# Routing of an attention-then-experts kernel: two-operand work moved from VectorE to GpSimd or PSUM, and a new order of the last head pair

## The chip, the cores and the metric

The kernel runs on one core of a Trainium2 chip. The core has a matrix engine (TensorE, PE), a vector engine (VectorE, DVE), an activation engine (ScalarE, ACT), GpSimd (POOL) and a DMA queue that SyncE issues (SP). All run their own instruction queue in order and wait for each other by semaphores. The metric is device time of one execution in microseconds.

## The reference, cut to what matters

```python
# attention: 4 batches, 8 heads, 768 tokens, 64 dims; a query sees only keys with the same 6-bit hash
mask = q_bucket[:, :, :, None] == k_bucket[:, :, None, :]
scores = where(mask, scale * q @ k.T, -1e9)
attn_out = softmax(scores) @ v                      # -> x of 3072 tokens x 512
# mixture of experts: 8 experts, the best one of each token
logits = x @ w_gate
expert_idx = argmax(logits, axis=1)
gate_w = softmax(logits)[arange(N), expert_idx]
# for each expert e: y[its tokens] = relu(x[its tokens] @ w1[e]) @ w2[e]
return gate_w[:, None] * y
```

The argmax takes the first of equal logits, and the weight of the chosen expert is 1 over the sum of exp(logit - maximum).

## The kernel before, in words

**Stages.** Attention runs over 16 pairs of heads (4 batches of 4 pairs), then the experts run as dense matrix products over rows that were sorted by expert in DRAM. A pair's work is cut into named steps, and a table of tokens sets their order: `HEAD` for the first pair, `PLAN` for each of the next 14, `LAST` for the sixteenth. All engines get their instructions in the order of the tokens, so a token that waits on an engine holds all later tokens of that engine.

**Tokens.** A token's digits name a unit; each trailing `-` means the pair before. `S` scores (PE, into a PSUM bank named `s`, 3 banks), `R` minimum and copy of the scores (DVE, L307), `X` exponential (ACT, L313), `T` four transposes on PE (L327) into a bank named `t` (2 banks, shared by `T`, `V`, `K`, `G` and routing), `E` their eviction (`a` on ACT, `v` on DVE), `V` product with the values (PE, L389, 24 instructions), `O` its eviction (ACT, L395), `M` the reciprocal sums (DVE), `K` tokens and logits (PE, L409), `L` their scaling into the row buffer `xr` (DVE, L419), `D` half the transposes of the weights on DVE (L349), `G` the hash products of the next pair (PE, L254), `H` their signs (ACT), `N` the load of the hash masks (two DMAs issued by POOL, L270), `P0` to `P7` the split of the next pair's queries and keys into a high and a low part (POOL, L190 to L200). The scores of a pair need the masks and the split parts that the pair before it made.

**Routing.** A batch's four pairs give the logits (summed over pairs in L441). `route` then finds the maximum, the first index that has it, a one-hot row `oh`, and on PE (L460 to L463) running counts that give each token its slot in the sorted rows. Batches 0 to 2 route all six token tiles in one generator, a step at a time: `route_step` runs steps 1 to 6 behind the `R` tokens of the second pair of the next batch (from `L0--` on: `R0 R3 R11 R10 R5 R4`), steps 7 and 8 at `G` of its third pair, two more behind the first `R`s there. The last batch runs in two halves of three tiles inside `LAST`, by tokens `r0` and `r1`; its result decides the order of experts.

**The end of attention.** In `LAST` POOL (and a little ACT) also splits the first expert's weights, 16 parts of a cast (`n`) and a subtraction (`t`), some by tokens and some behind `R` tokens; two raw buffers are loaded by SP after each second subtraction. `x0` and `x2` transpose 256 early rows of the first expert, `g` and `h` evict them to a high (ACT) and a low part (DVE, L755), `m0` to `m7` are the first product with those rows (PE, L772, 12 matmuls each), `u` and `d` its ReLU and low part, `c0` and `c1` the scatter of the last batch's rows (POOL). Each `m` reads the quarters of `x0` first and those of `x2` from its seventh matmul on.

Of the kernel before, what the change touches and what calls it, by code (L numbers as in the profile page):

```python
# [7 lines left out]
F32 = mybir.dt.float32  # L8
# [23 lines left out]
M0 = float(2 ** 34)  # L32
# [22 lines left out]
def lsh_attention_moe(ctx, tc, qk, qk2, v, proj, wg, w1, w1p, w2, out):  # L55
    nc = tc.nc
    const = ctx.enter_context(tc.tile_pool(name="const", bufs=1))
    moe = ctx.enter_context(tc.tile_pool(name="moe", bufs=1))
    ps = ctx.enter_context(tc.tile_pool(name="ps", bufs=1, space=bass.MemoryType.PSUM))
    ctx.enter_context(tc.manual_schedule())  # L60
    attn = ExitStack()
    wk = attn.enter_context(tc.tile_pool(name="wk", bufs=2))
# [73 lines left out]
    C = {}  # L136
# [244 lines left out]
    PV, RC, OT, LT, XR = {}, {}, {}, {}, {}  # L381
# [47 lines left out]
    def route(b, hfs):

        nt = 3 * len(hfs)
        l = wk.tile([128, 2, 2 * 3, E], F32, name="rl")
        lg, eq = l[:, 0, :nt], l[:, 1, :nt]
        f = wk.tile([128, 3, 2 * 3], F32, name="rf")
        mx, fi, sm = f[:, 0, :nt], f[:, 1, :nt], f[:, 2, :nt]
        oh = C["oh"] if nt > 3 else C["ohs"][:, hfs[0]]
        ex = C["ex"][:, 3 * hfs[0]:3 * hfs[0] + nt]
# [21 lines left out]
        p = ps.tile([128, 512], F32, name="t", bufs=2)  # L459
# [5 lines left out]
        yield  # L465
        pb = wk.tile([128, 2 * 3 + 1, E], F32, name="pb")
        nc.vector.tensor_tensor(pb[:, :nt + 1], p[:, :(nt + 1) * E].rearrange("p (t e) -> p t e", e=E),
                                C["base"][:, None, :].to_broadcast([128, nt + 1, E]), op=OP.add)
        C["base"] = pb[:, nt]
        pb = pb[:, :nt]  # L470
        yield
        nc.vector.tensor_tensor(pb, pb, oh[:, :nt], op=OP.mult)
        slot = wk.tile([128, 2 * 3], I32, name="slot")
        with nc.allow_low_precision("whole numbers below 2**24"):
            nc.vector.tensor_reduce(slot[:, :nt], pb, axis=AX.X, op=OP.add)
        yield
        nc.vector.tensor_reduce(sm, ex, axis=AX.X, op=OP.add)
        for i, hf in enumerate(hfs):
            nc.vector.reciprocal(XR[b, hf][:, :, GC], sm[:, 3 * i:3 * i + 3])
            SL[b, hf] = slot[:, 3 * i:3 * i + 3]  # L480
        yield

    def scatter(b, hf):
# [297 lines left out]
    M1 = {}  # L781
# [104 lines left out]
    routes, parts, pick = {}, list(range(16)), pick_first()  # L886
# [10 lines left out]
    def weight_half(op, x):  # L897
# [48 lines left out]
    steps = dict.fromkeys(range(B - 1), 0)  # L946

    def on(b, n):
        for _ in range(n):
            next(routes[b], None)  # L950
            steps[b] += 1

    def route_step(g, w, k):

        b, q = divmod(g - NP, NP)
        if 0 <= b < B - 1 and w[0] == "R" and q == 1 and {(g - 2, "L0"), (g - 2, "L1")} <= DONE and steps[b] < 6:
            if b not in routes:
                routes[b] = route(b, (0, 1))
# [44 lines left out]
    def step(g, w):  # L1003
# [173 lines left out]
    with tc.If(C["n"] > 0):  # L1177
        with tc.For_i(0, C["n"], 1) as i:
# [16 lines left out]
            p = ps.tile([128, 512], F32, name="t", bufs=2)  # L1195
# [5 lines left out]
            for f in range(8):  # L1201
                p = ps.tile([128, 512], F32, name="t", bufs=2)
# [3 lines left out]
            p = ps.tile([128, 512], F32, name="s", bufs=3)  # L1206
# [34 lines left out]
```

## Time and profile before

| | us |
|---|---|
| median of 3 timed runs | 717.16 (716.2 to 717.37) |
| profiled execution, its own time | 715.56 |
| its span, first to last instruction | 713.7 |
| PE busy in the span | 695.7 |
| DVE, ACT, POOL busy | 454.3, 434.9, 469.0 |
| mean granted TensorE clock | 0.993 |

The profile is of one execution. "Busy" of PE means that an instruction was in flight, so a PE that runs at half clock is busy too. The span stands 1.9 us under that execution's own time, and its own time 1.6 us under the median of the timed runs.

### The profile page before, as it was taken

Reading aid. Unit: us, or ns where it says so; the run is one execution under the profiler, and the core shown is the slowest. Engines: PE = TensorE matmul, PEld = TensorE weight load, DVE = VectorE, ACT = ScalarE, POOL = GpSimd, SP = SyncE. Lnnn points to the kernel's source line nnn. Section 1 sums busy time; section 2 is a strip of 40 time slices with the busy share of each in tenths; the row PEclk is TensorE's granted clock in tenths of the full one; section 3 lists DMA queues with packets and bytes.
Section 4 is the critical chain, followed back from the end, with each engine's and each line's share of the span. In section 5 each row is a group of like instructions: output and inputs, shape, how many; then the busy total and the mean of one; then the engine's idle time right before and its main releaser. Section 6 shows DMA issues by size and latency. Waiting matters only on the chain.

```text
span 713.7 us, 12263 instructions
## 1 busy us (share of the span) xinstructions
PE 695.7 (97%) x4219; PEld 568.3 (80%) x4219; DVE 454.3 (64%) x924; ACT 434.9 (61%) x864; POOL 469.0 (66%) x507
## 2 busy tenths in 40 slices
PE   9999999899999999998999799999999999999997
PEld 5777768667686668676876599899999999989896
DVE  8878777977788878788864632641848534262521
ACT  7988788668888788887866214543444444444320
POOL 7966855565796658874967704766656667768432
PEclk9999999899999999999999999999999999999999
DMA  8519867866888448865875218584537495637201
GB/s 306 130 53 247 223 208 215 219 160 213 258 234 225 130 135 227 220 201 117 241 236 186 100 65 227 174 229 128 162 113 186 137 114 214 192 133 215 75 11 40
DMA packets 64528, 123.09 MB, mean 172 GB/s; under 512 B 15331, under 2 KB 29027, under 8 KB 64400
## 3 DMA queue, kind: packets, MB, share of 16 engines
q1 hardware_dynamic: 56736, 103.17, 52.1%
q0 software_dynamic: 7584, 19.10, 8.5%
q8 instruction: 34, 0.56, 0.3%
q14 instruction: 30, 0.25, 0.1%
q10 hardware_dynamic: 144, 0.02, 0.0%
HBM read 65.75 MB, written 26.33 MB: 129 GB/s over the span
## 4 chain that ended last, share of the span: by engine, by line
PE 89%; issue 4%; DVE 3%; ACT 1%; POOL 1%; DMA 0%; POOLq 0%; ACTq 0%; DVEq 0%
PE s L772 18%; PE t L389 18%; PE s L809 10%; PE s L297 10%; PE t L327 10%; PE s L299 9%; PE s L829 8%; PE t L409 3%; PE t L254 2%; PE s L838 1%; DVE e L307 1%; POOL w L668 1%; DVE rl L448 1%; PE t L103 1%; ACT e L313 0%
## 5 line engine op out<-in xcount | busy, mean ns | idle before, releaser
L307 DVE TENSOR_SCALAR_CACHE_REDUCE e<-s 128x768 f32<-128x768 f32 x192 | 178.7, 954 | 62.0 <-PE s L299 54.5
L313 ACT ACTIVATE e<-e,m 128x768 f32<-128x768 f32 x192 | 177.9, 930 | 17.4 <-DVE e L307 14.8
L668 POOL TENSOR_TENSOR w<-raw,w 128x512 fp32r<-128x512 f32 x112 | 144.7, 1319 | 38.7 <-ACT w L667 38.2
L389 PE MATMUL t<-pt,vt 128*64 128x384 f32 x768 | 131.3, 491 | 0.0
L772 PE MATMUL s<-xh,w 128*128 128x456 f32 (+6 forms) x672 | 126.8, 346 | 0.0
L772 PEld LDWEIGHTS s<-xh,w 128*128 128x128 f32 x672 | 119.2, 188 | 3.1
L788 DVE SCALAR_TENSOR_TENSOR hh<-s,hh 128x256 fp32r<-128x256 f32 (+7 forms) x64 | 35.5, 555 | 110.7 <-ACT hh L786 103.8
L389 PEld LDWEIGHTS t<-pt,vt 128*64 128x64 f32 x768 | 52.4, 137 | 64.3 <-issue 63.2
L327 PE MATMUL t<-ident,e 128*128 128x128 f32 x648 | 93.5, 276 | 3.9 <-DVE xr L419 2.7
L379 ACT ACTIVATE pt<-t 128x512 f32<-128x512 f32 (+1 forms) x149 | 83.3, 582 | 19.4 <-PE t L327 18.2
L327 PEld LDWEIGHTS t<-ident,e 128*128 128x128 f32 x648 | 77.6, 142 | 11.7 <-issue 4.4
L786 ACT ACTIVATE hh<-s 128x256 fp32r<-128x256 f32 (+7 forms) x64 | 31.4, 490 | 88.5 <-PE s L772 83.5
L349 DVE STREAM_TRANSPOSE w<-e 128x768 f32<-128x768 f32 x84 | 79.2, 965 | 0.2 <-ACT e L313 0.2
L809 PE MATMUL s<-hh,w 128*128 128x456 f32 (+3 forms) x384 | 74.9, 355 | 0.0
L809 PEld LDWEIGHTS s<-hh,w 128*128 128x128 f32 x384 | 71.1, 188 | 2.6
L667 ACT ACTIVATE w<-raw 128x512 fp32r<-128x512 f32 x112 | 66.3, 622 | 6.5 <-DMA raw<-in_w1p_dram 6.5
L845 POOL DMA_INDIRECT out_dram<-y,ix x26 | 25.9, 997 | 61.7 <-DVE y L843 30.9
L297 PE MATMUL s<-w 80*128 80x384 f32 x192 | 56.2, 374 | 2.9 <-DVE e L307 2.9
L829 PE MATMUL s<-w,hh 128*128 128x512 f32 (+1 forms) x240 | 56.4, 394 | 0.0
L297 PE MATMUL s<-qk 80*128 80x384 f32 x192 | 54.8, 367 | 0.0
L829 PEld LDWEIGHTS s<-w,hh 128*128 128x128 f32 (+1 forms) x240 | 44.6, 187 | 10.5
L299 PE MATMUL s<-w 128*128 128x384 f32 x192 | 50.1, 342 | 0.0
(206 smaller groups left out, 995.0 us busy)
## 6 DMA issues: line engine op xcount, KB each, us to landing
pt<-w SPq DMA_DIRECT2D x224, 144.0 KB
raw<-in_w_dram SPq DMA_DIRECT2D x36, 512.0 KB
raw<-in_w1p_dram SPq DMA_DIRECT2D x28, 512.0 KB
xd<-in_qk_dram SPq DMA_DIRECT2D x14, 768.0 KB
sorted_rows<-xr SPq DMA_DIRECT2D x6, 1156.0 KB
vt<-in_v_dram SPq DMA_DIRECT2D x16, 384.0 KB
masks<-bits POOLq DMA_DIRECT2D x14, 192.0 KB, 3.9
sorted_rows<-sorted_rows SPq DMA_DIRECT2D x2, 1156.0 KB
```

The source lines that it names most:

```text
L297: nc.tensor.matmul(p[:, a, :HALF], k[0:80, 2, c], k[0:80, 3, n], start=i >= 4, stop=i < 4)
L299: nc.tensor.matmul(p[:, a, :HALF], k[:, 0, c], k[:, 1, n], start=i < 4, stop=i >= 4)
L307: nc.vector.tensor_scalar(e, SC.pop(i)[:, :, :HALF], CEIL, None, op0=OP.min, op1=OP.min, accum_out=m)
L313: nc.scalar.activation(e, e, AF.Exp, bias=m, scale=-1.0, accum_out=SM[g, hf][:, t, s:s + 1])
L327: nc.tensor.transpose(o[:, j, w], e[w][:, kt // 3, (kt % 3) * 128:(kt % 3) * 128 + 128], ident)
L349: nc.vector.transpose(z[:, :, c, w].rearrange("p g (k i) -> p g k i", i=32), e)
L379: nc.scalar.activation(o, x, AF.Copy)
L389: nc.tensor.matmul(p[s * 64:(s + 1) * 64, :HALF], VT[g][:, kt, s, :], PT[u][:, :, :, s, kt].rearrange("p a t i -> p t a i"), start=(kt == ...
L668: nc.gpsimd.tensor_tensor(w[:, 1, a], r, w[:, 0, a], op=OP.subtract)
L772: nc.tensor.matmul(p[:, :c], w[:, a, d, fs], x[:, b, d, :c], start=(k == 0), stop=(k == 11))
L809: nc.tensor.matmul(p[:, :c], w[:, a, f % 4, ms], h[b][:, f, :c], start=(k == 0), stop=(k == 23))
L829: nc.tensor.matmul(p[:pw], HH[n][b][:, f, i:i + pw], w[:, a, f % 4], start=(k == 0), stop=(k == 23))
```

## The change

Batches 0 to 2: `route` gives to POOL every step that combines two SBUF operands. The one-hot row comes from a subtraction and a comparison with zero (`zero`) in place of a comparison of two tensors. Five small instructions go to POOL behind the maximum and behind `fi`, and one (`pb` times `oh`) behind the counts; DVE keeps the reductions and the addition that reads PSUM. The exponential and the counts stand at `G`, and the steps are one more.

The last batch: `route_last` keeps all on DVE and puts the logits, `eq` and `fi` in the unused part of the counts' PSUM bank, so that each two-operand instruction has one operand in PSUM.

`LAST` is a new table of the same work: `x2 g2 h2 m6 m1` move ahead of `L1` and `r1`, the half that pair 15 finishes first is `K0 L0`, `K1` stands right behind `V1`, two subtractions of the weights move from POOL to DVE (`tV`), and one part of the weights to the end.

```diff
+        def zero(o, x):
+            G.tensor_scalar(o, x, 0.0, 1.0, op0=OP.is_equal, op1=OP.mult)
+        logits(b, 0, lg[:, 0:3])
+        yield
+        logits(b, 1, lg[:, 3:6])
         nc.vector.tensor_reduce(mx, lg, axis=AX.X, op=OP.max)
-        nc.vector.tensor_tensor(eq, lg, bc(mx), op=OP.is_equal)
-        nc.vector.tensor_tensor(eq, eq, dsc, op=OP.mult)
+        yield
+        G.tensor_tensor(lg, lg, bc(mx), op=OP.subtract)
+        zero(eq, lg)
+        G.tensor_tensor(eq, eq, dsc, op=OP.mult)
+        yield
+        yield
+        yield
         nc.vector.tensor_reduce(fi, eq, axis=AX.X, op=OP.max)
-        nc.vector.tensor_tensor(oh[:, :nt], dsc, bc(fi), op=OP.is_equal)
-        (nc.gpsimd if many else nc.vector).tensor_tensor(lg, lg, bc(mx), op=OP.subtract)
+        G.tensor_tensor(eq, dsc, bc(fi), op=OP.subtract)
+        zero(oh[:, :nt], eq)
         yield
         nc.scalar.activation(ex[:, :, 0:E], lg, AF.Exp)
-        yield
         p = ps.tile([128, 512], F32, name="t", bufs=2)
+        counts(p, oh, nt)
+        yield
...
+        C["base"] = pb[:, nt]
+        G.tensor_tensor(pb[:, :nt], pb[:, :nt], oh[:, :nt], op=OP.mult)
...
+    def route_last(b, hf):
+        nt = 3
+        p = ps.tile([128, 512], F32, name="t", bufs=2)
+        part = [p[:, (nt + 1 + i) * E * nt:(nt + 2 + i) * E * nt].rearrange("p (t e) -> p t e", e=E) for i in range(3)]
+        lg, eq = part[:2]
+        fi = part[2][:, :, 0]
...
+        logits(b, hf, lg)
+        V.tensor_reduce(mx, lg, axis=AX.X, op=OP.max)
+        yield
+        V.tensor_tensor(eq, lg, bc(mx), op=OP.is_equal)
+        V.tensor_tensor(eq, eq, dsc, op=OP.mult)
+        V.tensor_reduce(fi, eq, axis=AX.X, op=OP.max)
+        V.tensor_tensor(oh[:, :nt], dsc, bc(fi), op=OP.is_equal)
+        yield
+        V.tensor_tensor(l, lg, bc(mx), op=OP.subtract)
+        nc.scalar.activation(ex[:, :, 0:E], l, AF.Exp)
+        yield
+        counts(p, oh, nt)
...
+        V.tensor_tensor(q[:, :nt], q[:, :nt], C["base"][:, None, :].to_broadcast([128, nt, E]), op=OP.add)
+        V.tensor_tensor(q[:, :nt], q[:, :nt], oh[:, :nt], op=OP.mult)
+        slots(b, (hf,), q[:, :nt])
...
     LAST = """
-        r0 r0 r0 r0 r0 r0 c0 x2 O1 K1 L1 r1 r1 r1 r1 r1 r1 r1 c1 g2 h2 m6 m3 u3 d3 m2 u2 d2 m7 u6 d6 u7 d7 m1 u1 d1 m4
+        R7 E42a T50 E50a T52 E52v K0 L0 nP tV x0 X7 T31 E31a T30 T32 E30a M1 E32v K0- g0 h0 V1 O1 K1 nP tP nA tP L0-
+        r0 r0 r0 r0 r0 r0 c0 x2 g2 h2 m6 u6 m1 u1 L1 r1 r1 r1 r1 r1 d6 r1 c1 d1 m7 u7 d7 m3 u3 d3 m4 u4 d4 m2 u2 d2 m0
...
-            elif w[0] == "R" and 8 <= steps[b] < 10:
+            elif w[0] == "R" and 8 <= steps[b] < 11:
                 on(b, 1)
```

DVE in the second pair of the second batch, between the logits and the eviction that follows; L307 is an `R`, L349 a `D`, L419 an `L`. Before:

```order
L441 TENSOR_REDUCE rl<-xr 128x24
L349 STREAM_TRANSPOSE w_1587<-e 128x4x192 x3
L307 TENSOR_SCALAR e,m<-s 128x768
L444 TENSOR_REDUCE rf<-rl 128x6
L445 TENSOR_TENSOR rl<-rl,rf 128x48
L307 TENSOR_SCALAR e,m<-s 128x768
L448 TENSOR_TENSOR rl<-rl,desc 128x48
L451 TENSOR_REDUCE rf<-rl 128x6
L419 TENSOR_TENSOR xr<-t,r 128x3x144
L307 TENSOR_SCALAR e,m<-s 128x768
L454 TENSOR_TENSOR oh<-desc,rf 128x48
```

And after the change, in the same place:

```order
L477 TENSOR_REDUCE rl<-xr 128x24
L446 TENSOR_REDUCE rf<-rl 128x6
L349 STREAM_TRANSPOSE w_1588<-e 128x4x192 x3
L307 TENSOR_SCALAR e,m<-s 128x768 x2
L419 TENSOR_TENSOR xr<-t,r 128x3x144
L307 TENSOR_SCALAR e,m<-s 128x768 x2
L454 TENSOR_REDUCE rf<-rl 128x6
```

L445, L448 and L454 left DVE; of the rows that remain only L419 has two operands, and one of them (`t`) is in PSUM. The maximum comes earlier, and the reduction to `fi` stands two `R`s later.

POOL in the same pair, from the last cast before the masks to the pair's end: before (the first three rows of the split, then the routing's one subtraction, the masks and the low parts `P3 P2 P7`):

```order
L198 TENSOR_TENSOR qk<-xd,qk 64x768
L194 CAST qk<-xd 64x768
L196 COPY qk<-qk 64x768
L455 TENSOR_TENSOR rl<-rl,rf 128x48
L270 DMA qk<-masks 16x4x384 x2
L200 TENSOR_TENSOR qk<-xd,qk 64x768
L198 TENSOR_TENSOR qk<-xd,qk 64x768
L200 TENSOR_TENSOR qk<-xd,qk 64x768
L194 CAST w_1790<-xd 64x768
```

After:

```order
L198 TENSOR_TENSOR qk<-xd,qk 64x768
L448 TENSOR_TENSOR rl<-rl,rf 128x48
L441 TENSOR_SCALAR rl<-rl 128x48
L450 TENSOR_TENSOR rl<-rl,desc 128x48
L194 CAST qk<-xd 64x768
L196 COPY qk<-qk 64x768
L455 TENSOR_TENSOR rl<-desc,rf 128x48
L441 TENSOR_SCALAR oh<-rl 128x48
L270 DMA qk<-masks 16x4x384 x2
L200 TENSOR_TENSOR qk<-xd,qk 64x768
L198 TENSOR_TENSOR qk<-xd,qk 64x768
L200 TENSOR_TENSOR qk<-xd,qk 64x768
```

Three small instructions stand behind the maximum, and two behind `fi`; the masks and the three low parts stand behind those two. Behind the last L200 follows the product of `pb` and `oh`, ahead of the next pair's first cast.

PE at the end of attention, from the last `V` on (L389 is `V1`, L409 a `K`, L460 and L463 the counts, L751 is `x2`, L772 an `m`); before:

```order
L327 MATMUL t<-ident,e 128x4x32 x12
L409 MATMUL t<-wgt,ot 128x144 x3
L389 MATMUL t<-pt,vt 64x384 x12
...
L463 MATMUL t<-ohs,ones 128x8
L751 MATMUL s<-ident,xd 128x128 x4
L409 MATMUL t<-wgt,ot 128x144 x3
...
L463 MATMUL t<-ohs,ones 128x8
L772 MATMUL s<-xhe,w_4428 128x256 x12
```

After (the counts are L480 and L482, `x2` is L801, an `m` L822):

```order
L327 MATMUL t<-ident,e 128x4x32 x12
L409 MATMUL t<-wgt,ot 128x144 x3
L389 MATMUL t<-pt,vt 64x384 x12
L409 MATMUL t<-wgt,ot 128x144 x3
...
L482 MATMUL t<-ohs,ones 128x8
L801 MATMUL s<-ident,xd 128x128 x4
L822 MATMUL s<-xhe,w_4401 128x256 x12
L822 MATMUL s<-xhe,w_4308 128x256 x12
...
L482 MATMUL t<-ohs,ones 128x8
L822 MATMUL s<-xhe,w_4401 128x256 x12
```

`K1` moved ahead of the first half's counts, and two `m`s (24 matmuls) stand between the two counts where `K1` alone stood.

## Rows read from the trace of the kernel before

**Rows 1.** Waits of PE: waited for, us in total, times, longest us.

```profile
PE s L297 <- DVE e L307: 2.9, 2, 1.6
PE t L460 <- DVE ohs L454: 2.8, 2, 2.4
PE t L327 <- DVE xr L419: 2.7, 1, 2.7
PE s L772 <- DVE xhe L755: 1.1, 1, 1.1
```

**Rows 2.** The chain in order of time: start us, us, what (`V1`, `G`, `V0`).

```profile
102.39 4.02 PE t L389 x24
118.91 0.78 PE t L254 x8
125.47 4.02 PE t L389 x24
154.85 4.02 PE t L389 x24
238.16 4.02 PE t L389 x24
242.75 0.85 PE t L254 x8
318.60 4.02 PE t L389 x24
344.20 4.02 PE t L389 x24
```

**Rows 3.** Windows: us, PE, PEld, DVE, ACT, POOL busy, PE clock, DMA, GB/s.

```profile
137.00:144.00 7.00, 6.04 (x24) 5.24 (x26) 6.04 (x14) 4.47 (x10) 2.62 (x2) 0.51 0.36 79
407.00:410.00 3.00, 2.60 (x12) 2.60 (x13) 0.35 (x1) 0.00 (x0) 2.18 (x5) 0.50 0.52 190
```

**Rows 4.** Tile rl: DVE's product, duration ns min/median/max, first and last start.

```profile
L448 DVE TENSOR_TENSOR rl<-rl,desc x5: 182/205/4169, 132.9 to 404.3; 128x48 f32<-128x48 f32 x3, 128x24 f32<-128x24 f32 x2
L455 POOL TENSOR_TENSOR rl<-rl,rf x3: 268/268/270, 131.9 to 325.0; 128x48 f32<-128x48 f32 x3
```

**Rows 5.** Timeline of DVE and POOL in batch 2's routing: start us, us.

```profile
328.03 2.60 DVE L454 TENSOR_TENSOR oh<-desc,rf 128x48 bf16<-128x48 f32 x1
...
326.90 1.86 POOL L200 TENSOR_TENSOR qk<-xd,qk 64x768 fp32r<-64x768 f32 x1
328.71 1.83 POOL L198 TENSOR_TENSOR qk<-xd,qk 64x768 fp32r<-64x768 f32 x1
```

**Rows 6.** Timeline of a pair without routing: DVE's `R4`, POOL's `N`.

```profile
111.77 0.95 DVE L307 TENSOR_SCALAR_CACHE_REDUCE e<-s 128x768 f32<-128x768 f32 x1
...
105.30 1.02 POOL L270 DMA_DIRECT2D w<-masks  x2
```

**Rows 7.** The masks' load, line 270: us from issue to landing.

```profile
DMA to landing us min/median/max: 3.2/4.1/4.6
```

**Rows 8.** Timeline of the last pair's end, each engine: start us, us.

```profile
389.18 4.00 PE L327 MATMUL t<-ident,e 128*128 128x128 f32 x24
407.40 12.18 PE L772 MATMUL s<-xhe,w 128*128 128x256 f32 x89 [1.14 <-DVE xhe L755]
...
389.29 0.49 ACT L395 ACTIVATE ot<-t 128x384 f32<-128x384 f32 x1 [1.13 <-PE t L389]
405.19 0.58 ACT L753 ACTIVATE xhe<-s 128x512 fp32r<-128x512 f32 x1
...
406.67 0.68 DVE L755 TENSOR_TENSOR xhe<-s,xhe 128x512 fp32r<-128x512 f32 x1
...
377.65 0.61 POOL L908 CAST w<-raw 128x512 fp32r<-128x512 f32 x1 [4.72 <-DMA raw<-in_w_dram]
399.48 1.27 POOL L665 TENSOR_TENSOR w<-raw,w 128x512 fp32r<-128x512 f32 x1
...
374.87 0.89 SPq L694 DMA_DIRECT2D xd<-sorted_rows  x2
```

More of the change, by code (lines that the diff above doesn't have):

```diff
@@ L427, in bc, with route @@
         return ap[:, :, None].to_broadcast([128, ap.shape[1], E])
[L429 to L431 removed]
+    def route(b):
+        nt = 6
         l = wk.tile([128, 2, 2 * 3, E], F32, name="rl")
[L433 removed]
+        lg, eq = l[:, 0], l[:, 1]
         f = wk.tile([128, 3, 2 * 3], F32, name="rf")
[L435 to L437 removed]
+        mx, fi, sm = f[:, 0], f[:, 1], f[:, 2]
+        oh, ex = C["oh"], C["ex"]
@@ L458, in route @@
+        counts(p, oh, nt)
         yield
-        p = ps.tile([128, 512], F32, name="t", bufs=2)
+        pb = wk.tile([128, 2 * 3 + 1, E], F32, name="pb")
+        nc.vector.tensor_tensor(pb, p[:, :(nt + 1) * E].rearrange("p (t e) -> p t e", e=E),
+                                C["base"][:, None, :].to_broadcast([128, nt + 1, E]), op=OP.add)
+        C["base"] = pb[:, nt]
+        G.tensor_tensor(pb[:, :nt], pb[:, :nt], oh[:, :nt], op=OP.mult)
+        yield
+        nc.vector.tensor_reduce(sm, ex, axis=AX.X, op=OP.add)
@@ L460, in route, with logits, counts @@
+        for i in range(2):
+            nc.vector.reciprocal(XR[b, i][:, :, GC], sm[:, 3 * i:3 * i + 3])
+        yield
+        yield
+        slots(b, (0, 1), pb[:, :nt])
+        yield
+    def logits(b, hf, o):
+        nc.vector.tensor_reduce(o, XR[b, hf][:, :, :GC].rearrange("p t (a x e) -> p t e a x", a=NP, e=E)[:, :, :, :, 0:PW // E:PW // E - 1], axis=AX.XY, op=OP.add)
+    def counts(p, oh, nt):
         nc.tensor.matmul(p[:, :(nt + 1) * E], C["tri"], oh, start=True, stop=False)
@@ L464, in route, with slots @@
                              start=False, stop=(t == nt - 1))
[L465 to L472, printed above, removed]
+    def slots(b, hfs, pb):
@@ new lines, in slots @@
+        for i, hf in enumerate(hfs):
+            SL[b, hf] = slot[:, 3 * i:3 * i + 3]
+    def route_last(b, hf):
+        nt = 3
+        p = ps.tile([128, 512], F32, name="t", bufs=2)
+        part = [p[:, (nt + 1 + i) * E * nt:(nt + 2 + i) * E * nt].rearrange("p (t e) -> p t e", e=E) for i in range(3)]
+        lg, eq = part[:2]
+        f = wk.tile([128, 3, 2 * 3], F32, name="rf")
+        mx, sm = f[:, 0, :nt], f[:, 2, :nt]
+        fi = part[2][:, :, 0]
+        l = wk.tile([128, 2, 2 * 3, E], F32, name="rl")[:, 0, :nt]
+        oh = C["ohs"][:, hf]
+        ex = C["ex"][:, 3 * hf:3 * hf + nt]
+        dsc = C["desc"][:, None, :].to_broadcast([128, nt, E])
+        V = nc.vector
+        logits(b, hf, lg)
+        V.tensor_reduce(mx, lg, axis=AX.X, op=OP.max)
+        yield
+        V.tensor_tensor(eq, lg, bc(mx), op=OP.is_equal)
+        V.tensor_tensor(eq, eq, dsc, op=OP.mult)
+        V.tensor_reduce(fi, eq, axis=AX.X, op=OP.max)
+        V.tensor_tensor(oh[:, :nt], dsc, bc(fi), op=OP.is_equal)
+        yield
+        V.tensor_tensor(l, lg, bc(mx), op=OP.subtract)
+        nc.scalar.activation(ex[:, :, 0:E], l, AF.Exp)
+        yield
+        counts(p, oh, nt)
+        yield
+        q = p[:, :(nt + 1) * E].rearrange("p (t e) -> p t e", e=E)
+        if hf == 0:
+            pb = wk.tile([128, 2 * 3 + 1, E], F32, name="pb")
+            V.tensor_tensor(pb[:, nt], q[:, nt], C["base"], op=OP.add)
+        V.tensor_tensor(q[:, :nt], q[:, :nt], C["base"][:, None, :].to_broadcast([128, nt, E]), op=OP.add)
+        if hf == 0:
+            C["base"] = pb[:, nt]
+        V.tensor_tensor(q[:, :nt], q[:, :nt], oh[:, :nt], op=OP.mult)
+        slots(b, (hf,), q[:, :nt])
+        yield
+        V.tensor_reduce(sm, ex, axis=AX.X, op=OP.add)
+        V.reciprocal(XR[b, hf][:, :, GC], sm)
@@ L957, in route_step @@
             if b not in routes:
[L958 removed]
+                routes[b] = route(b)
             on(b, 1)
@@ L1091, in step @@
             weight_half(op, x)
-    last = [route(B - 1, (0,)), route(B - 1, (1,))]
+    last = [route_last(B - 1, 0), route_last(B - 1, 1)]
     for g in range(NG):
```

26 lines of the change are left out of this document (6 added, 20 removed).

## The prediction

> **What bounds the kernel now.** PE does: in the table of times it is busy in all but 18 us of the span, so I look for places where it is not, or where it runs slowly. The list of what PE waited for comes first [rows 1]. The reader is to see that its longest entries all name DVE, and among them instructions of routing or ones that stand right behind routing: 2.9 us in two waits, 2.7 in one, 2.8 and 1.1 at the end of attention. Next comes the chain in order of time, which gives the price of a pair [rows 2]: from one `V1` to the next an ordinary pair takes 125.47 - 102.39 = 23.08 us, the pair with batch 0's routing 154.85 - 125.47 = 29.38, that of batch 2 25.60. Third are the windows with the granted clock [rows 3]: behind the 2.7 us wait PE runs 7 us at the lower level (0.51 of 2.4 GHz), and again from 407 to 410, behind the two waits at the end. Last comes the tile view, which says what DVE was doing [rows 4]: one 48-element product, 0.205 us in the median of five, lasted 4.17 us once. The timeline beside it [rows 5] shows the like in batch 2: L454 lasts 2.60 us, from 328.03 to 330.63, and POOL's second subtraction ends at 330.54. So a DVE instruction with two SBUF operands sits until POOL lets go, the `R` and `L` tokens queue up behind it, the PSUM banks stay full and PE stops. Elsewhere no engine holds PE for long, so only these places can move the end.
>
> **Batches 0 to 2.** The change takes L445, L448, L454 and the product of `pb` and `oh` from DVE, that is, every DVE instruction of these batches that has two SBUF operands. What PE gets back, from the periods: batch 0, 29.38 - 23.08 = 6.30; batch 2, 25.60 - 23.08 = 2.52; batch 1, whose wait is the other of the two (2.9 - 1.6 = 1.3) where batch 2's is 1.6, by the same difference about 2.2. Not all of it goes: the counts still stand at `G` and still hold its bank until DVE adds the base. `V0` of batch 1 starts at 238.16, lasts 4.02, and `G` starts at 242.75: 0.57 us each [rows 2]. The gain is 6.30 + 2.2 + 2.52 - 3 x 0.57 = 9.3 us. In batch 0 about 3.4 of this is clock, 7.0 x 0.49 [rows 3], which comes back if the 2.7 us wait goes.
>
> What DVE keeps is no more than it had: two reductions to logits, a maximum, the reduction to `fi`. What POOL gets is six instructions of 48 elements, and one like them takes 0.268 us [rows 4], 1.6 us per batch on an engine with idle time in each pair. The cost hides if the work behind them is not late, and here a new wait is added: POOL's second group waits for `fi`, which stands behind `R4`, and the mask loads and the low parts `P3 P2 P7` are queued behind it; the next pair's first scores need them. In a pair without routing `R4` ends at 111.77 + 0.95 = 112.72 [rows 6]; a period later that is 135.8, and `fi` is there at 136.0 (0.2, as for a product of 48 elements [rows 4]). Then two small instructions with their semaphores, 0.8; two mask issues, 1.02; `P3` 1.86 and `P2` 1.83 [rows 5, 6]: 141.5. The masks land at most 4.6 us behind an issue [rows 7]: the second, issued at about 137.4, at 142.0. The scores come behind `G`: 118.91 + 23.08 + 0.57 + 0.78 = 143.3 [rows 2]. Cover: 1.8 us for the parts, 1.3 for the masks. Without routing POOL issues the masks at 105.30 + 23.08 = 128.4, so 8.5 us of cover go. I cost this at nothing, with a high end of 1 us per batch (small POOL instructions with half a microsecond of overhead each). At `G`, POOL's product waits for `pb`, and the next pair's first cast and scaling stand behind it; these have a whole pair ahead.
>
> **The last pair.** The table moves tokens and leaves PE's matmuls as they are. What goes: the waits for `ohs` (2.8) and `xhe` (1.1) [rows 1], and the low clock behind them, 3.0 x 0.5 = 1.5 [rows 3], 5.4 us in all. What comes in its place, by PE's new order:
> - `K1` stands right behind `V1`, so it waits for the eviction `O1`: it begins 0.11 behind the end of a `V`, lasts 0.49 [rows 8], and with its semaphore makes 0.65 us. Before, the first half's counts and `x2` lay there.
> - The first half's counts: their chain runs on DVE under `V1` (4.02 us), as long as `r1`'s chain, which is the 2.4 us wait [rows 1], and more. No wait.
> - `m6` behind `x2`: `g2` (0.58) and then `h2` (0.68) [rows 8], with two semaphores about 1.45, under seven matmuls of 12.18 / 89 = 0.137, 0.96. A wait of 0.5.
> - `r1` behind `h2`: 2.4 us of chain under 17 matmuls, 2.3 us. A wait of 0.2 with its semaphore.
> - `tV`, a subtraction of two SBUF operands of 128 x 512 on DVE, once at the start of the pair and once at `K0 L0`. The first lies under `V1-`. For the second, POOL must have cast part 12. Its last twelve parts run from 377.65 to 400.75 [rows 8], 1.925 each; in the new table eight of them precede, then the cast: 377.65 + 15.4 + 0.6 = 393.7, and up to 0.9 later since SP now issues the row loads [rows 8] ahead of the raw loads. DVE reaches it at about 394: `K0` and `L0` follow the 24 transposes that end at 393.2 [rows 8]. So `tV` meets POOL's next cast (0.61) and the subtraction behind it (1.27), and the eviction that `V1` needs for its bank is queued behind `tV`. Nothing at best, 1.9 at worst; I take 0.6, the cast alone: the subtraction behind it waits for that cast, so the port comes free between them.
>
> New waits 0.65 + 0.5 + 0.2 + 0.6 = 1.95, so the last pair gives 5.4 - 1.95 = 3.4 us (1.5 to 4.5). Which subtraction holds DVE for how long is not settled by these rows: L454 asked at 328.03 while L200 ran until 328.76, and was let in only when the next, L198, had ended at 330.54 [rows 5]; POOL went first although it asked later. The Trainium skill (SBUF — State Buffer, "Who interferes with whom") has it that the shared port pair is held for one whole instruction by whichever of the two began first. By that rule `tV` loses no more than the running instruction and the term stays 0.6; by the row it can lose two, which makes it 1.9 and the forecast 705.7. The row is the measurement, so the upper end stays in the range.
>
> **What hides nothing.** The four waits shown are the longest of that list, and none of them lies in the experts' part behind; its loads hang on the counts of `r1`, which end no later against `m5` than before; a shorter attention moves it as a whole. So the sum reaches the end: 9.3 + 3.4 = 12.7. The profiled execution's own time is 715.56, which gives 702.9. The median of the timed runs is 1.6 above it, and I apply the same difference to that: 717.16 - 12.7 = 704.4.
>
> **The rivals.**
> - *The last pair gives nothing.* `tV` takes 1.9, the waits behind `x2` and `r1` come out at 1.5 together, and the clock falls all the same since PE stops three times in 8 us: 5.4 - 0.65 - 1.9 - 1.5 - 1.5 = -0.1. Then 717.16 - 9.3 = 707.9. For it: two waits of 2.4 and 1.1 were enough for the lower clock. Against: the new waits are under 1 us each and have matmuls between them.
> - *GpSimd's chain is a little late in each batch.* 1 us per batch: 717.16 - 12.7 + 3 = 707.5. For it: 8.5 us of cover shrink to 1.3. Against: each duration in that chain is a row.
> - *GpSimd's chain becomes the bound, and the kernel is slower.* If the masks or `P2` come 2.7 us behind `G` in each batch, PE stops as long as it did in batch 0 and loses the clock likewise: 2.7 + 3.4 = 6.1 in each, 18.3 against 9.3, less 3.4: 722.8. The point from which the kernel is slower is a loss of 12.7 / 3 = 4.2 us in each batch; with the clock that takes a chain 1.3 + 2.7 = 4.0 us longer than I worked out. For it: POOL's spans of small instructions are rough, and POOL now waits for DVE twice per batch. Against: the two instructions behind `fi` would have to take 2 us each, where L455 took 0.27.
> - *The change does not do what it says.* DVE still stops, now at `fi`, for POOL's first group. Those three stand 8 us ahead of `fi` (three `R`s and an `L`) and take about 1 us, so PE's waits would have another cause than the port. Then batches give nothing: 717.16 - 3.4 = 713.8, or no change if the last pair fails too.
>
> **How the numbers follow.** Forecast 0.58, with its own range of 702 to 706.5; last pair nothing 0.18; a little late 0.12; no effect in the batches 0.06 (half of it within the bound); slower 0.05; 0.01 is left. The likeliest is 704.4. The range of 702 to 709 takes in the first three cases. A measurement of this kernel can tell about 0.2% (1.4 us) from no change: faster by more 0.91, within 0.04, slower 0.05.
>
> **What would show it.** Right: no DVE instruction of routing over 0.3 us in the three batches; periods of 23.7 us there; the clock at 1.00 from 130 to 400; PE's waits for `ohs` gone, in their place one of about 0.6 for `ot` and one of about 0.5 for `xhe`. Wrong: a PE wait in the first scores behind `G` on masks or on POOL's low parts (the second and third rival); `tV` over 1.3 us with `V1` waiting for an eviction, or a clock of 0.5 in the last 15 us of attention (the first); a DVE wait at `fi` (the fourth). I would be wrong as a whole if PE's time came from matmuls that are slower in the new order, which no row here shows.

## The result, and the profile after

The changed kernel takes 708.94 us (median; 707.85 to 709.86), the kernel before 717.06 in the runs beside it. The ratio is 0.9888 (0.9871 to 0.9905): 8.1 us faster. The forecast was 704.4, 4.5 us too fast; the rival "the last pair gives nothing" had 707.9.

The profiled run took 709.86 us (span 708.1). What PE waited for (us in total, times, longest):

```profile
PE t L389 <- DVE pt L377: 2.8, 1, 2.8
...
PE t L254 <- ACT qk L237: 1.0, 1, 1.0
PE t L254 <- DVE pb L463: 0.9, 3, 0.3
PE t L480 <- DVE rl L514: 0.7, 1, 0.7
PE t L409 <- ACT ot L395: 0.7, 1, 0.7
...
PE s L822 <- DVE xhe L805: 0.3, 1, 0.3
```

Of the four entries of [rows 1], `e` and `xr` are gone and `xhe` fell from 1.1 to 0.3. Of the two waits for `ohs` the second half's, 2.4, is gone; the first half's stays under another name (L480) and is 0.7 where it was 0.4. A wait as long as the longest of them has come: `V1` (L389) waits 2.8 us for an eviction by DVE (L377). `K1` (L409) is a smaller new one. The three waits for `pb` (the base added at `G`) were 0.9 us before, too.

The chain in order of time gives the price of the pairs (start us, us, what), as in [rows 2]:

```profile
103.18 4.02 PE t L389 x24
...
126.26 4.02 PE t L389 x24
...
150.00 4.02 PE t L389 x24
...
219.26 4.02 PE t L389 x24
...
242.99 4.02 PE t L389 x24
...
312.25 4.02 PE t L389 x24
...
336.10 4.02 PE t L389 x24
```

Each pair with routing now takes 23.7 to 23.9 us from `V1` to `V1` (150.00 - 126.26 = 23.74, then 23.73 and 23.85), where batch 0's took 29.38. With three marks the whole span can be shared out between the two profiles. The third mark is the first matmul of the experts' second product (L829 before, L879 after); its rows are:

```profile
419.42 6.93 PE L829 MATMUL s<-w,qk 128*128 128x512 f32 x29
```

```profile
413.91 10.43 PE L879 MATMUL s<-w,qk 128*128 128x512 f32 x44
```

| stretch | before | after | gain |
|---|---|---|---|
| start to the first `V1` shown | 102.39 | 103.18 | -0.79 |
| from it to the last batch's `V1` of the chain (344.20, 336.10) | 241.81 | 232.92 | 8.89 |
| from there to the second product | 75.22 | 77.81 | -2.59 |
| the rest of the span (713.7, 708.1) | 294.28 | 294.19 | 0.09 |

So the three batches gave nearly what was forecast (8.9 of 9.3), and the last pair, with 3.4 forecast, lost 2.6. The first row has nothing to do with the edit: at the start, an instruction that is the same in both kernels (DVE L218, at 9.3) took 0.55 us in the one execution and 1.40 in the other, and PE's wait for `qk` (L237), 1.0 above, was 0.2 in the profile before.

What DVE and POOL now do for routing, from the tile view of `rl` (durations in ns min/median/max, first and last start):

```profile
L446 DVE TENSOR_REDUCE rf<-rl x3: 203/203/204, 128.3 to 314.3; 128x6 f32<-128x48 f32 x3
...
L454 DVE TENSOR_REDUCE rf<-rl x3: 197/198/200, 136.5 to 322.6; 128x6 f32<-128x48 f32 x3
L455 POOL TENSOR_TENSOR rl<-desc,rf x3: 267/267/268, 136.9 to 322.9; 128x48 f32<-128x48 f32 x3
```

In place of the 4.17 us product of [rows 4] each of these has the same length three times: none of them is held any more. The windows of [rows 3] have moved (us, busy time of PE, PEld, DVE, ACT, POOL, then PE's clock, DMA share, GB/s):

```profile
137.00:144.00 7.00, 6.69 (x51) 3.53 (x49) 5.77 (x14) 5.59 (x13) 6.82 (x7) 1.00 0.36 113
...
390.40:397.30 6.90, 5.98 (x20) 2.33 (x22) 1.94 (x5) 0.00 (x0) 1.12 (x1) 0.52 0.15 58
```

The low clock (1.2 of 2.4 GHz) in batch 0 is gone. Its like now stands in the last pair, behind `V1`'s wait. The timeline there shows why `V1` waits (start us, us, instruction, in brackets the idle time ahead of it and what ended it):

```profile
373.45 0.61 POOL L714 CAST w<-raw 128x512 fp32r<-128x512 f32 x1 [12.11 <-DMA raw<-in_w_dram]
...
385.54 0.61 DVE L419 TENSOR_TENSOR xr<-t,r 128x432 f32<-128x432 f32 x1 [0.34 <-PE t L409]
...
387.55 1.00 PE L409 MATMUL t<-wgt,ot 128*128 128x144 f32 x6
388.70 1.16 POOL L958 CAST w<-raw 128x512 fp32r<-128x512 f32 x2
389.34 1.06 DVE L964 TENSOR_TENSOR w<-raw,w 128x512 fp32r<-128x512 f32 x1 [3.19 <-POOL w L958]
...
390.61 0.65 DVE L377 COPY pt<-t 128x512 f32<-128x512 f32 x1
...
391.32 6.92 PE L389 MATMUL t<-pt,vt 128*64 128x384 f32 x24 [2.77 <-DVE pt L377]
...
398.89 1.00 PE L409 MATMUL t<-wgt,ot 128*128 128x144 f32 x6 [0.65 <-ACT ot L395]
...
400.64 0.19 PE L480 MATMUL t<-ohs,tri 128*128 128x32 bf16 x1 [0.75 <-DVE rl L514]
...
402.81 2.29 PE L822 MATMUL s<-xhe,w 128*128 128x256 f32 x17 [0.28 <-DVE xhe L805]
```

From the top: POOL begins its run of weight parts at 373.45, when the raw weights have landed. DVE is through with `L0` (L419) at 386.15 and comes to the second `tV` (L964), whose cast by POOL (L958) is the ninth part and begins at 388.70. DVE stands for 3.19 us. Queued behind it is the eviction of PSUM (L377) that `V1` needs. `V1` starts 2.77 us late and lasts 6.92 us instead of 4.09, since the clock has fallen. The lines below it are the smaller waits of the new order. SP's queue shows what the raw loads stand behind:

```profile
366.65 0.90 SPq L744 DMA_DIRECT2D xd<-sorted_rows  x2
367.80 9.92 SPq L704 DMA_DIRECT2D raw<-in_w_dram  x3
```

In the kernel before, the first raw load had been issued ahead of the row loads (L694, at 374.87 in [rows 8]); now they precede it:

```profile
374.03 0.39 SPq L654 DMA_DIRECT2D raw<-in_w_dram  x1
```

### The profile page after: what moved, and what is told of

Same layout as the page of the kernel before. It is cut to its first block, busy times and chain, and to the rows that moved or that the text cites. A ratio compares the mean times of both kernels' runs of the same rounds, so it can differ in the third digit from the quotient of the medians.

```text
span 708.1 us, 12282 instructions
## 1 busy us (share of the span) xinstructions
PE 694.2 (98%) x4219; PEld 566.5 (80%) x4219; DVE 446.7 (63%) x916; ACT 433.6 (61%) x863; POOL 470.7 (66%) x520
## 4 chain that ended last, share of the span: by engine, by line
PE 90%; issue 4%; POOL 2%; ACT 1%; DVE 1%; DMA 0%; POOLq 0%; ACTq 0%
PE t L389 19%; PE s L822 18%; PE s L859 10%; PE s L297 10%; PE s L299 9%; PE t L327 9%; PE s L879 8%; PE t L409 3%; PE t L254 2%; PE s L888 1%; POOL w L718 1%; PE t L103 1%; POOL w L715 0%; ACT e L313 0%; DMA out_dram<-e,ix 0%
## 5 line engine op out<-in xcount | busy, mean ns | idle before, releaser
L307 DVE TENSOR_SCALAR_CACHE_REDUCE e<-s 128x768 f32<-128x768 f32 x192 | 178.7, 953 | 61.4 <-PE s L299 52.4
L389 PE MATMUL t<-pt,vt 128*64 128x384 f32 x768 | 133.7, 499 | 2.8 <-DVE pt L377 2.8
L822 PE MATMUL s<-xh,w 128*128 128x456 f32 (+6 forms) x672 | 126.8, 346 | 0.0
L822 PEld LDWEIGHTS s<-xh,w 128*128 128x128 f32 x672 | 119.2, 188 | 3.0
L389 PEld LDWEIGHTS t<-pt,vt 128*64 128x64 f32 x768 | 53.4, 139 | 68.4 <-issue 63.4
L327 PE MATMUL t<-ident,e 128*128 128x128 f32 x648 | 92.0, 274 | 1.3 <-DVE pt L377 0.5
L379 ACT ACTIVATE pt<-t 128x512 f32<-128x512 f32 (+1 forms) x148 | 82.3, 581 | 13.7 <-PE t L327 12.3
L349 DVE STREAM_TRANSPOSE w<-e 128x768 f32<-128x768 f32 x84 | 79.1, 964 | 0.8 <-DMA pt<-w 0.6
L879 PE MATMUL s<-w,hh 128*128 128x512 f32 (+1 forms) x240 | 56.4, 394 | 0.0
L879 PEld LDWEIGHTS s<-w,hh 128*128 128x128 f32 (+1 forms) x240 | 44.7, 187 | 10.4
L299 PE MATMUL s<-qk 128*128 128x384 f32 x192 | 49.8, 341 | 0.0
```

The source lines that it names most:

```text
L299: nc.tensor.matmul(p[:, a, :HALF], k[:, 0, c], k[:, 1, n], start=i < 4, stop=i >= 4)
L307: nc.vector.tensor_scalar(e, SC.pop(i)[:, :, :HALF], CEIL, None, op0=OP.min, op1=OP.min, accum_out=m)
L327: nc.tensor.transpose(o[:, j, w], e[w][:, kt // 3, (kt % 3) * 128:(kt % 3) * 128 + 128], ident)
L349: nc.vector.transpose(z[:, :, c, w].rearrange("p g (k i) -> p g k i", i=32), e)
L379: nc.scalar.activation(o, x, AF.Copy)
L389: nc.tensor.matmul(p[s * 64:(s + 1) * 64, :HALF], VT[g][:, kt, s, :], PT[u][:, :, :, s, kt].rearrange("p a t i -> p t a i"), start=(kt == ...
```

## The experiments

Theory A: the second `tV` alone spoils the last pair (a cast that comes late, an eviction queued behind, the clock). Theory B: the last pair's other new waits, or its order as a whole, do. For the lateness and for the port there were theories of their own. In the diffs, lines of the table `LAST` are cut to the tokens around the edit. Where a kernel builds on tv2_on_pool and not on the changed kernel, its first line says so.

**tv2_on_pool**: the second subtraction goes back to POOL.

```diff
-        ... K0 L0 nP tV x0 X7 ...
+        ... K0 L0 nP tP x0 X7 ...
```

> The changed kernel with the second tV (DVE's subtraction of weight part 12) given back to POOL as a tP, and nothing else. Theory A (DVE stood 3.2 us at that subtraction for a cast that POOL had not made yet, the eviction that V1 needs was queued behind it, and the 2.8 us wait then cost the clock): the 2.8 us wait of PE for pt and the 6.8 us at the lower clock behind it go, about 2.8 + 3.4 less some 0.6 that other waits take: 703 to 705. Rival B (the end of attention is held by something later, such as the chain from V1's eviction to the counts, and tV only hides it): 708 to 709, with PE's wait moved to the counts. Both: batch periods stay at 23.7.

704.22 us, ratio 0.9835 (0.9815 to 0.9856). In its timeline:

```profile
388.24 1.00 PE L409 MATMUL t<-wgt,ot 128*128 128x144 f32 x6
388.44 0.69 DVE L377 COPY pt<-t 128x512 f32<-128x512 f32 x1 [1.12 <-PE t L327]
...
389.19 4.09 PE L389 MATMUL t<-pt,vt 128*64 128x384 f32 x24
...
408.94 10.44 PE L879 MATMUL s<-w,qk 128*128 128x512 f32 x44
```

The eviction runs as soon as PE has filled the bank, `V1` follows `K0-` (L409) without a wait and runs at the full clock (mean 1.000 over the profile). One token is worth 708.94 - 704.22 = 4.7 us by the medians (3.8 by the two ratios; 5.9 against the changed kernel's repeat below, 710.16). In the profiles it is 5.7: from `K0-` to `V1` 3.77 against 0.95, and from `V1` to the second product (413.91, 408.94) 22.59 against 19.75. This kernel beats both.

**early_only**: the new routing in batches 0 to 2; the last batch with the routing and the table of before.

```diff
+    def route_old(b, hfs):     # route of the kernel before, for the last batch
...
-     LAST = """ ... (new) """
+     LAST = """ ... (before) """
```

> The kernel before with the new routing of batches 0 to 2 alone (GpSimd's six instructions, the new steps); the last batch's routing and the table of the last pair are those of before. Prediction's term for the batches, 9.3 us: 707.8, with periods of 23.7 us and no DVE wait there; the end of attention as before (waits of 0.4, 2.4 and 1.1 us and the low clock behind). Rival C (the profile's pairs overstate it, since the low clock behind batch 0 was peculiar to that run): 711 to 712.

708.01 us, ratio 0.9882 (0.9853 to 0.991): 8.55 us from the batches alone. Its last pair keeps the waits of before and shows the clock at 0.52 behind them:

```profile
397.10 0.18 PE L564 MATMUL t<-ohs,tri 128*128 128x32 bf16 x1 [2.31 <-DVE ohs L558]
```

```profile
398.00:404.90 6.90, 6.31 (x30) 6.01 (x29) 1.51 (x7) 0.39 (x1) 3.97 (x9) 0.52 0.55 208
```

**last_only**: the reverse, the routing of before in batches 0 to 2, with `route_last` and the new `LAST`.

```diff
-     LAST = """ ... (before) """
+     LAST = """ ... (new) """
+    def route_last(b, hf):
```

> The changed kernel with the routing of batches 0 to 2 as before; the new table of the last pair and the routing of the last batch with operands in PSUM stay. Theory A (the last pair lost 1 to 3 us by the wait for tV and the clock): 717.5 to 720. The prediction's own term (3.4 us gained) would be 713.7.

717.18 us, ratio 1.0016 (1.0002 to 1.003). The two halves of the change are worth 8.55 and about nothing, together 7.9 against 8.1 measured. `V1` waits here too, somewhat shorter, and this time the clock holds:

```profile
397.97 1.06 DVE L1018 TENSOR_TENSOR w<-raw,w 128x512 fp32r<-128x512 f32 x1 [2.52 <-POOL w L1012]
...
399.95 4.09 PE L389 MATMUL t<-pt,vt 128*64 128x384 f32 x24 [2.08 <-DVE pt L377]
```

In this profile the stretch from the chain's last `V1` (345.49) to the second product (419.71) is 74.22 us against 75.22 before, so 1.0 was gained. That the ten timed runs show none of it is not explained by one profile. With the routing of before, DVE's holds of [rows 4] and [rows 5] come back at the same places, 4.18 and 2.60 us long.

**rows_later**: `tV` stays; the loads of the first expert's rows are issued one `R` later, behind the first two raw loads.

```diff
-        if g == NG - 1 and w[0] == "R" and k < 3:
+        if g == NG - 1 and w[0] == "R" and k < 4:
...
-            if k == 2:
+            if k == 3:
```

> The changed kernel with SP's loads of the first expert's sorted rows issued one R token later, so behind the raw loads that tV and the next two subtractions trigger and not ahead of them. Theory A with its cause (raw loads issued late and landing together with the rows made POOL's chain start 3.9 us late): POOL's wait for raw falls from 12 us to 8 to 10, the second tV ends 2 to 3 us earlier, V1's wait falls below 1 us and the clock holds: 703.5 to 706. Rival B' (tV is held by the shared port and POOL's next instructions, not by a late cast): no more than 0.5 us off the changed kernel.

704.98 us, ratio 0.9848 (0.9827 to 0.9869). SP, POOL and PE:

```profile
366.64 1.01 SPq L704 DMA_DIRECT2D raw<-in_w_dram  x2
368.10 0.90 SPq L744 DMA_DIRECT2D xd<-sorted_rows  x2
...
370.88 0.61 POOL L714 CAST w<-raw 128x512 fp32r<-128x512 f32 x1 [9.57 <-DMA raw<-in_w_dram]
...
388.96 4.09 PE L389 MATMUL t<-pt,vt 128*64 128x384 f32 x24 [0.54 <-DVE pt L377]
```

The raw loads go out 1.16 us earlier and land faster: POOL begins 4.24 us behind the first issue, where it was 373.45 - 367.80 = 5.65. POOL's run moves 2.57 us ahead, and `V1`'s wait shrinks from 2.77 to 0.54. So the place of two row loads in SP's queue made most of `tV`'s lateness.

**tv2_behind_e32**: `tV` stays on DVE and the loads as they were; `tV` moves behind the last evictions, and `L0-` with them.

```diff
-  ... K0 L0 nP tV x0 X7 T31 E31a T30 T32 E30a M1 E32v K0- g0 h0 V1 O1 K1 nP tP nA tP L0- r0 ...
+  ... K0 L0 nP x0 X7 T31 E31a T30 T32 E30a M1 E32v K0- g0 h0 L0- tV V1 O1 K1 nP tP nA tP r0 ...
```

> The changed kernel with the second tV left on DVE but moved behind E32v, h0 and L0- (L0- moves ahead with it), so behind the eviction that V1 needs. Theory A (what cost was the place in DVE's queue, ahead of that eviction, and not the subtraction): V1's wait and the low clock go, DVE's wait for the cast lies under V1: 703.8 to 705. Rival (DVE and POOL delay each other at the shared port wherever it stands): POOL's chain and the counts slip, over 706.

704.84 us, ratio 0.9832 (0.9807 to 0.9857).

```profile
389.25 4.09 PE L389 MATMUL t<-pt,vt 128*64 128x384 f32 x24
390.36 1.07 DVE L964 TENSOR_TENSOR w<-raw,w 128x512 fp32r<-128x512 f32 x1
```

The same subtraction costs nothing under `V1`. What cost was its place ahead of an eviction that PE needs, not its work on DVE.

**no_tv**: both subtractions by POOL (on tv2_on_pool).

```diff
-        ... R4 X4 tV V1- S8 ...
+        ... R4 X4 tP V1- S8 ...
```

> The kernel with both tV on POOL. If the first tV was hidden under V1- as I worked out, it is the same within 0.5 us: 703.8 to 704.8. If POOL was the slower place for it, since it triggers a raw load, POOL's chain starts later and PE waits for pt or the counts: over 705.

705.06 us, ratio 0.9839 (0.9823 to 0.9856), the same span in the profile as tv2_on_pool (703.1). The median is 0.84 above tv2_on_pool's and in the range of the second case, but the ratios differ by only 0.0004 (0.3 us), so whether the first `tV` helps a little can't be told.

**oh_on_dve2**: DVE makes the one-hot of batches 0 to 2 again, from two SBUF operands (on tv2_on_pool).

```diff
-        G.tensor_tensor(eq, dsc, bc(fi), op=OP.subtract)
-        zero(oh[:, :nt], eq)
+        nc.vector.tensor_tensor(oh[:, :nt], dsc, bc(fi), op=OP.is_equal)
```

> The kernel with the second tV on POOL, and in batches 0 to 2 the one-hot row made by DVE again, by one comparison of two SBUF operands of 48 elements behind fi; GpSimd's other instructions stay. Port theory: POOL, which no longer waits for fi, is in its last low part when DVE asks, and the comparison takes 1 to 2 us in place of 0.2 in two or three of the batches; PE waits 0 to 1.5 us in each: 704.5 to 708. Rival (what the batches lost was the number of DVE instructions): 0.2 us each, 704.2 or less.

706.05 us, ratio 0.9849 (0.9832 to 0.9865), 1.8 us more than tv2_on_pool by the medians and 1.0 by the ratios, with overlapping intervals. DVE's instruction and POOL's beside it:

```profile
136.45 1.83 POOL L200 TENSOR_TENSOR qk<-xd,qk 64x768 fp32r<-64x768 f32 x1
...
136.81 1.55 DVE L455 TENSOR_TENSOR oh<-desc,rf 128x48 bf16<-128x48 f32 x1
```

A 48-element comparison takes 1.51 to 1.55 us in all three batches, and it ends when L200 does (138.36 against 138.28). PE's wait at `G` is then 0.90 in each batch in place of 0.31: 3 x 0.59 = 1.8. Between the chain's first and last `V1` shown, the profiles differ by the same 1.8 (234.71 against 232.94). This is the batches' mechanism, put back alone.

**r0_under_v1**: half of `r0` ahead of `O1` and `K1` (on tv2_on_pool).

```diff
-        ... h0 V1 O1 K1 nP tP nA tP L0- r0 r0 r0 r0 r0 r0 c0 ...
+        ... h0 L0- V1 r0 r0 r0 O1 K1 nP tP nA tP r0 r0 r0 c0 ...
```

> The kernel with the second tV on POOL, and the tokens L0- and the first three r0 (logits to exponential of the last batch's first half) moved ahead of O1 and K1; nothing else. Theory D (with its operands in PSUM the chain of r0 needs a bank named t, and K1 had taken the only one free, so the chain waited for V1's eviction): the chain now takes the bank that L0- frees, runs under V1, and PE's 0.74 us wait at the counts goes: 703.3 to 703.7 where that kernel had 704.2. Rival (the chain waits for L0- on DVE): the wait stays, 704.2.

704.31 us, ratio 0.9818 (0.9802 to 0.9834).

```profile
390.58 0.52 DVE L477 TENSOR_REDUCE t<-xr 128x24 f32<-128x192 f32 x1
```

```profile
395.07 0.18 PE L480 MATMUL t<-ohs,tri 128*128 128x32 bf16 x1
```

The chain (L477) now runs under `V1`, and the counts' wait is gone; from `V1` to the second product it is 18.94 us (389.49 to 408.43) against 19.75. The gain of 0.8 is in the trace, and in the medians it can't be told from nothing.

**x2_under_o1**: `x2` between `O1` and `K1` as well, to hide `K1`'s wait (on tv2_on_pool).

```diff
-        ... V1 O1 K1 nP tP nA tP L0- r0 r0 r0 r0 r0 r0 c0 x2 g2 h2 m6 ...
+        ... L0- V1 r0 r0 r0 O1 x2 g2 h2 K1 nP tP r0 r0 r0 c0 nA tP m6 ...
```

> The same, with x2, g2 and h2 between V1's eviction O1 and K1, and POOL's part 14 behind c0. If PE's waits at K1 (0.65), the counts (0.74) and m6 (0.28) are each what the order around V1 makes, x2 (0.45) fills the first, and g2 and h2 lie under K1: 702.5 to 703.2. If they only move to the next place (r1's counts or m7): 703.5 to 704.

704.41 us, ratio 0.9828 (0.9812 to 0.9844). Missed: `K1` no longer waits, but the second half's counts now do (0.60), and an `m` for its bank (0.60). The time moved on and did not go.

**warm_under_wait, warm8, changed_again**: the changed kernel with 11 or 8 matmuls of ones (512 columns, their result unused) between `K0-` and `V1`, and the changed kernel itself once more beside warm8.

```diff
-        ... K0- g0 h0 V1 O1 K1 ...
+        ... K0- g0 h0 i11 V1 O1 K1 ...
...
+            if g == NG - 1:
+                warmth(ps.tile([128, 512], F32, name="s", bufs=3), int(x))
```

> The changed kernel with eleven matmuls of ones (128x512, bf16, about 0.21 us each, into a bank of s that nothing reads) on PE between K0- and V1, where PE waits for the second tV. They do no work of the computation. If the wait of 2.8 us costs its own length and then as much again by the lower clock: V1 still waits (0.3 to 0.6 us behind the dummies), the clock stays at 1.00, V1 lasts 4.1 and not 6.9 us: 705 to 706.5. Rival (the clock falls for another reason, such as the table's order as a whole): V1 lasts 6.9 again, 708.5 to 709.5.

> The changed kernel with eight matmuls of ones between K0- and V1 (eleven had made V1 wait 0.5 us longer in the profile than without them). They do no work of the computation. If the clock is a steady part: a mean clock of 0.998 or more in each run, and a median 1.5 to 2.5 us below the kernel above, 706 to 707.5. If the clock costs nothing that is measured and V1's wait is all: the same as the kernel above within 0.7 us.

> The changed kernel as it is, beside the next one on the same chip, for the clock of each run. If the low clock behind V1's wait is a steady part of its time: a mean granted clock of 0.995 to 0.997 in each run and a median of 708 to 709.5.

warm_under_wait took 708.71 (ratio 0.989, 0.9866 to 0.9915); warm8 708.38 (0.9897, 0.9876 to 0.9919); changed_again 710.16 (0.9921, 0.9901 to 0.9941). In the profile of changed_again, and then of warm8:

```profile
390.73 5.70 PE L389 MATMUL t<-pt,vt 128*64 128x384 f32 x24 [2.83 <-DVE pt L377]
```

```profile
387.47 1.89 PE L103 MATMUL s<-ones 128*128 128x512 bf16 x8
...
390.38 4.09 PE L389 MATMUL t<-pt,vt 128*64 128x384 f32 x24 [1.02 <-DVE pt L377]
```

With the unused matmuls `V1` starts as late but lasts 4.09: a PE that is kept busy in the wait keeps the clock. The mean granted clock says the same: 0.994 to 0.997 in the six runs of changed_again, 0.997 to 1.000 in those of warm8. From the last batch's `V1` (335.36, 335.22) to the second product (412.21, 410.27) it is 76.85 us in changed_again's profile and 75.05 in warm8's, 1.8 less, of which `V1` itself is 1.6. The timed runs follow only in part, and both medians miss what was expected of the clock (705 to 706.5, and 706 to 707.5). warm8 is 1.8 us faster than changed_again, with overlapping intervals, and 11 matmuls, which make `V1` start 0.3 later behind `K0-` (4.11 against 3.77), gave 0.2 against the first 708.94. In the traces the low clock costs `V1` 1.6 to 2.8 us; how `tV`'s 4.7 us of the medians part into wait and clock stays open.

## Why the prediction was wrong

**The batches: right.** 9.3 us forecast, 8.9 between the marks of the two profiles, 8.55 by early_only. Three steps carried it. The periods were forecast as 23.7 (23.08 and 0.57) and came out at 23.74, 23.73 and 23.85, with `G`'s 0.57 as the part that stays. The port was the cause: oh_on_dve2 puts one two-operand instruction back and gets 1.5 us for it three times. And POOL's longer chain was costed at nothing with a cover of little over a microsecond; it held:

```profile
136.51 0.20 DVE L454 TENSOR_REDUCE rf<-rl 128x6 f32<-128x48 f32 x1
...
137.56 1.08 POOL L270 DMA_DIRECT2D qk<-masks  x2
...
140.44 1.83 POOL L198 TENSOR_TENSOR qk<-xd,qk 64x768 fp32r<-64x768 f32 x1
```

`fi` was worked out for 136.0, the masks' second issue for about 137.4, `P2`'s end for 141.5; with this profile's start 0.8 later they are 136.51, some 138.1 and 142.27, and PE's first scores behind `G` begin without a wait: PE's list has none for POOL or a DMA. The rivals in which GpSimd is late fall. One sign was put too narrowly: "no DVE instruction of routing over 0.3 us" left out the reductions to logits, which take 0.50 us in both kernels.

**The last pair's waits, but for `tV`: nearly right.** What goes was 5.4 us, and it went, but for the first half's counts. `K1` was put at 0.65 and is 0.65; `m6` behind `x2` at 0.5 and is 0.28; `r1`'s counts at 0.2 and show none. One step failed in a small way: "The first half's counts: their chain runs on DVE under `V1`". They wait 0.75, where they had waited 0.42 before. The chain doesn't run under `V1`: its operands lie in a PSUM bank `t`, the table puts `r0` behind `O1` and `K1`, and in tv2_on_pool DVE sits 3.66 us ahead of the chain's first instruction until ACT has evicted `V1`'s bank. With the tokens ahead of `O1` (r0_under_v1) the wait is gone. The port had no part in the longer wait for `ohs`: before, each two-operand instruction of the second half's chain took 0.18 us, and PE waited 2.37; in the first half's chain three were held (1.05, 0.52 and 1.10 us), and PE waited 0.42. So the new order took the long wait away, and what the operands in PSUM give by themselves no run separates. So these terms are 5.4 - 0.65 - 0.75 - 0.28 = 3.7, and tv2_on_pool's profile shows 75.22 - (408.94 - 336.89) = 3.2.

**`tV`: the step that failed.** It said "Nothing at best, 1.9 at worst; I take 0.6", and as a cost it weighed only the port. In the trace the port hardly matters there: `tV` itself lasts 1.06 us. DVE waited 3.19 us for its operand. The arrival of DVE was worked out well: 394, less the 9.3 of the batches and with the later start 385.5; it was through with `L0` at 386.15. The arrival of the cast was not: 393.7 and up to 0.9 later, in the same way 385.2 to 386.1, and it ended just ahead of 389.34. The working took over the 3.6 us from issue to use of the raw weights [rows 8] and allowed 0.9 for SP's row loads ahead of them; the loads went out 1.9 us later than that row carried over (374.03 in the trace before, less the measured 8.9 and plus 0.8, is 365.9; they went at 367.80), and took 5.65 us instead of 3.6. Half of the lateness is the queue, half the landing. rows_later takes away 2.57 us of it, and nearly all of the wait with it. "The eviction that `V1` needs for its bank is queued behind `tV`" stood in the same step, and tv2_behind_e32 shows that this alone made the lateness PE's; but the step priced the queue by the port, 1.9 at most, and left out the clock: a 2.8 us wait in one piece is as long as the one that had cost batch 0 its clock [rows 1, 3]. With 3.77 - 0.95 = 2.82 of wait and 22.59 - 19.75 = 2.84 behind it, nearly all in `V1`, the term is 5.7 us in the profile, 4.6 in that of changed_again (2.88 and 1.73) and 4.7 by the medians, against 0.6.

On the port itself the Trainium skill (SBUF — State Buffer, "SBUF: two separate sides") says that whichever of the two starts first has the shared pair for its whole instruction, and the other is blocked. Read so, DVE would lose no more than the running one. In oh_on_dve2 DVE asked at 136.81 and was let in as L200 ended at 138.28, which agrees, but POOL's next instruction came only at 144.11. In [rows 5] DVE also had to let the next one pass. In batch 0 its product is even recorded from before the first of two subtractions, and ends behind the second:

```profile
132.90 4.17 DVE L448 TENSOR_TENSOR rl<-rl,desc 128x48 f32<-128x48 f32 x1
...
133.38 1.86 POOL L200 TENSOR_TENSOR qk<-xd,qk 64x768 fp32r<-64x768 f32 x1
135.17 1.81 POOL L198 TENSOR_TENSOR qk<-xd,qk 64x768 fp32r<-64x768 f32 x1
```

So where POOL had more queued, the measurement goes against that bound. In both batches L198 is recorded to start just before L200 ends (135.17 against 135.24, 328.71 against 328.76), and DVE ends at the next gap between two of POOL's records (136.98 to 137.06, and 330.54 to 330.62). That it needs such a gap is a reading of rough spans and was not tested.

**The rivals.** "The last pair gives nothing" is nearest in time, but by another mechanism: `tV` cost more than its 1.9, by a late cast and not by the port; the clock fell behind one long wait and not behind three stops; and the waits behind `x2` and `r1` came out at 0.28, not 1.5. That its 707.9 lies near 708.94 is luck in part. last_only agrees in time: by itself, the new last pair is worth nothing. The offset between the profile and the median was 1.6, and it does not carry over, since here the profiled run is the longest of its four; the start of the kernel, which differs by 0.8 us between the two profiles, may be half of it, which no run shows. With the one token put back, the kernel takes 704.2. Without `tV`'s 0.6 the forecast would have been 703.8, a gain of 13.3; tv2_on_pool gains 8.9 + 3.2 = 12.1 between the marks of the profiles and 716.56 - 704.22 = 12.3 by the medians of the runs beside it. So the other terms held to about 1 us, and that 704.2 lies so near 704.4 is luck in part.

## What to carry to other kernels

Before an instruction is moved to an engine, work out when its operand is ready by the producer's own queue, from the load that starts it; then look at what stands behind it on the new engine and who needs that. A wait of an engine that runs ahead is free only while nothing that the bounding engine needs is queued behind it, and such an instruction belongs behind the last of these, not ahead. A new wait in one piece is to be priced with the clock of the trace if a wait of that size has cost it elsewhere.

## What the runs showed of the hardware

- The same load of raw weights took 3.6 us from issue to use before (374.03 to 377.65 [rows 8]; the next raw load went out 2.0 us later, at 376.03) and 3.8 in early_only with the same order, 4.24 in rows_later (two raw loads together, the row loads behind), and 5.65 in the changed kernel (the row loads ahead, two raw loads close behind each other). In the ten other profiles with the row loads ahead it took 5.1 to 6.6.
- Behind a wait in one piece of 2.77 or 2.83 us PE ran at half the clock for a while (`V1` 6.92 and 5.70 us), and behind 2.31 with 0.43 shortly before it too; behind 2.08 (last_only) it did not, nor behind 1.02 when PE had been kept busy until then (warm8).
- A reduction on DVE was not held by POOL: in oh_on_dve2 the reduction to `fi` took 0.20 us in all three batches while POOL's L200 was running (in batch 0 at 136.57, L200 from 136.45 to 138.28), and the two-operand comparison right behind it 1.51 to 1.55.
